# A transformer layer on one core: another way to the largest |k| of the first key block, with V copies and LayerNorm means moved between engines

## The chip, the cores and the metric

One core of a Trainium2 chip. The time is that of one execution in device microseconds; "before" is the median of three runs, 922.26 us (922.0 to 924.7). The durations quoted come from one profiled execution of 922.3 us, whose traced span is 920.3 us.

The engines by the names of the profile: PE is TensorE (PEld its weight loads), DVE is VectorE, ACT is ScalarE, POOL is GpSimd, SP is SyncE, which issues the DMAs here. All run their own instruction streams in order and wait for each other by semaphores.

## What is computed

One pre-norm transformer layer on 2048 tokens of width 640, in bfloat16: attention with 32 heads of 20 columns, then a gated feed-forward block of width 1728.

```python
h  = x + attention(layernorm(x), wqkv, wo)       # 32 heads, softmax over 2048 keys
h2 = h + (gelu(layernorm(h) @ w_gate) * (layernorm(h) @ w_up)) @ w_down

def attention(x, wqkv, wo):
    q, k, v = split(x @ wqkv)                    # each 2048 x 640
    p = softmax(q @ k.T * 20 ** -0.5)            # per head
    return concat(p @ v) @ wo
```

## The kernel before

**Planned order.** The kernel doesn't write out the order of its instructions. Every operation is handed to a planner (`Sched`, lines 44 to 295) with its engine, an estimated length, a priority, what it reads and writes, and the PSUM banks it takes and frees. The planner runs through time once and lets each free engine take the ready operation of the best priority; TensorE also gets filler matmuls where its recent load would be low. What comes out is one fixed stream per engine, with semaphore waits. So a changed length, priority or bank list can move instructions of all engines. Its estimates stand at the operations (`c_act(512)`, `c_dve(512)`, 0.33 and the like).

**Stages.** The work goes in three stages.

1. *Front.* x is loaded in four parts of four 128-token tiles. LayerNorm 1 (`ln_stats`, `act_stats`, `ln_rsqrt`, `ln_apply`, lines 532 to 633) gets mean and variance of a tile, on VectorE for three parts and on ScalarE for the second; `ln_rsqrt` rounds them to bfloat16 (`mv16`), adds epsilon (`sd16`), copies the mean to `mu`, takes a square root on ScalarE and a reciprocal (`rs`) on VectorE; `ln_apply` writes (x - mu) * rs on VectorE; `transposes` turns the tile over by five matmuls with the identity and copies it out of PSUM to `xnT`, on ScalarE except for tiles 13 and 15, which VectorE copies. Then come the projections. `proj_k(t)` makes block t of K (128 of the 640 columns, transposed, 6.4 heads) in four chunks c of 512 keys, five matmuls each; `proj_q(t, c)` the same for 512 queries; `proj_v(kt, hf)` the V rows of 128 keys for 16 heads.
2. *Attention.* Scores of four heads at a time (a head group), a tile of 128 keys x 512 query columns per head; ScalarE takes three or two such tiles in one exponential of 1536 or 1024 columns out of PSUM (lines 928 to 947); VectorE makes a few of the exponentials itself by arithmetic (`d_exp`, lines 833 to 873); TensorE sums over keys with V (`pv_op`, line 875). Queries go in seven parts of 512 to 128. K and Q blocks 1 to 4 and most of V are made during the first part, beside its exponentials.
3. *After each part of queries*: output projection, LayerNorm 2, feed-forward; for the last part nothing runs beside it (the tail).

**The bound on the scores.** The exponential needs a number to be subtracted per query. The kernel uses a bound: for each head the sum over its 20 rows of |q| times the largest |k| of that row over all keys. `kd[:, t]` holds this largest |k| of block t, `sel` a selector matrix (which row belongs to which head), scaled by `kd`. For the first block (t = 0) `sel0` takes the place of `sel`, and `q_bound0` (lines 749 to 759) multiplies it with |q| (line 752) and adds the result onto the q rows in `qt_all` (line 756). The first score matmul waits for that, and so does the first exponential.

In `proj_k(0)` (lines 674 to 714) each chunk is copied out of PSUM by ScalarE (line 667). VectorE then masks the sign bits of the copy (line 689), takes the running maximum of the chunks elementwise (line 694, from the second chunk on), after the last chunk halves the 512 columns to 256 by one more maximum (line 697), reduces these to one column (line 708) and scales `sel0` (line 711) and `sel` (line 713). For later blocks the masking is done once over 2048 columns and the halving goes 1024, 512, 256.

`proj_v(kt, 0)` is handed over for all 16 key tiles, in banks 6 and 7, its copies out of PSUM on VectorE (lines 1168 and 1169); the first four have a better priority than the others. K blocks from 1 on are copied on VectorE (line 670).

Most operations are recorded through the helper `I`, so their line in the profile is 354.

Of the kernel before, what the change touches and what calls it, by code (L numbers as in the profile page):

```python
# [7 lines left out]
ALU = mybir.AluOpType  # L8
# [291 lines left out]
D = 640  # L300
# [32 lines left out]
def bass_sequential_preLN__mha_block__glu_gated_geglu__prompt_kernel(  # L333
# [12 lines left out]
    with ExitStack() as es:  # L346
# [33 lines left out]
        sd16 = sb("sd16", [128, NT])  # L380
        nw = sb("nw", [128, 2, 4], FP32)
        kd = sb("kd", [128, NA], FP32)
        kt_all = sb("kt_all", [128, NG, S])
        qt_all = sb("qt_all", [128, 4, NG, 512])
        v_all = sb("v_all", [128, NT, H, VW])
# [142 lines left out]
        q_fills = [["qf0%d" % g for g in range(1, NG, 2)], ["qf1"], ["qf2"], ["qf3%d" % g for g in range(0, NG, 2)]]  # L528

        e_ops = []  # L530

        def ln_stats(src, t, rkeys, prio, after=()):
            s = t % 4
# [8 lines left out]
        def ln_rsqrt(t0, n, prio, table=False, sqrt=False):  # L542

            y = rs[:, t0:t0 + n]
            a, b = nw[:, 0, 0:n], nw[:, 1, 0:n]
            ts = range(t0, t0 + n)
            k16, ks = ("mv16", t0), ("sd16", t0)
            rk = [("rs", t) for t in ts]
            v = lambda fn, r, w: op("dve", fn, 0.17, prio, reads=r, writes=w)
            d = v if table or sqrt else lambda fn, r, w: op(POOL, fn, 0.25, prio, reads=r, writes=w)  # L550
            d(I("tensor_copy", mv16[:, t0:t0 + n, :], mv[:, t0:t0 + n, :]), [("mv", t) for t in ts], [k16])
            d(I("tensor_scalar", sd16[:, t0:t0 + n], mv16[:, t0:t0 + n, 1], LN_EPS, None, ALU.add), [k16], [ks])
            d(I("tensor_copy", mu[:, t0:t0 + n], mv16[:, t0:t0 + n, 0]), [k16], [("mu", t) for t in ts])
            if sqrt:
                op("act", I("activation", sd16[:, t0:t0 + n], sd16[:, t0:t0 + n], ACT.Sqrt), 0.2, 1, reads=[ks], writes=[ks])
                v(I("reciprocal", y, sd16[:, t0:t0 + n]), [ks], rk)
                return
            if table:
                op("act", I("activation", sd16[:, t0:t0 + n], sd16[:, t0:t0 + n], ACT.Sqrt), 0.2, -1, mode="sqrt", reads=[ks],
                   writes=[ks])  # L560
                v(I("reciprocal", y, sd16[:, t0:t0 + n]), [ks], rk)
                return
            d(I("tensor_copy", a, sd16[:, t0:t0 + n]), [ks], ["nw0"])
            d(I("tensor_scalar", y.bitcast(I32), a.bitcast(I32), -0.5, RSQRT_MAGIC, ALU.mult, ALU.add), ["nw0"], rk)
            for _ in range(2):
                d(I("tensor_tensor", b, y, y, ALU.mult), rk, ["nw1"])
                d(I("tensor_tensor", b, b, a, ALU.mult), ["nw0", "nw1"], ["nw1"])
                d(I("tensor_scalar", b, b, -0.5, 1.5, ALU.mult, ALU.add), ["nw1"], ["nw1"])
                d(I("tensor_tensor", y, y, b, ALU.mult), ["nw1"] + rk, rk)
            d(I("tensor_tensor", sd16[:, t0:t0 + n], a, y, ALU.mult), ["nw0"] + rk, [ks])  # L570
            v(I("reciprocal", y, sd16[:, t0:t0 + n]), [ks], rk)

        def ln_apply(eng, src, dst, dkey, t, rkeys, prio):
            if eng == "act":
                fn = I("activation", dst, src, ACT.Identity, bias=nm[:, t:t + 1], scale=rs[:, t:t + 1])
            else:
                fn = I("tensor_scalar", dst, src, mu[:, t:t + 1], rs[:, t:t + 1], ALU.subtract, ALU.mult)
            return op(eng, fn, 0.82 if eng == "act" else c_dve(D, 0.46), prio,
                      reads=list(rkeys) + [("mu", t), ("rs", t)] + ([("nm", t)] if eng == "act" else []), writes=[dkey])

        def transposes(src, rkeys, dst, wkey, banks, prio, evac, after=()):
# [40 lines left out]
        for t0 in (0, 4, 8, 12):  # L622
            if t0 == 4:
                act_stats(4, 4)
            else:
                for t in range(t0, t0 + 4):
                    ln_stats(x_sb[:, t, :], t, [f"x{t // 4}"], 1.4 if t0 == 12 else P_BG)
            ln_rsqrt(t0, 4, P_PRO, sqrt=True)
            for t in range(t0, t0 + 4):
                e_ops.append(ln_apply("dve", x_sb[:, t, :], xn_p[:, t % 4, :], ("xnp", t % 4), t, [f"x{t // 4}"], P_PRO))  # L630
                transposes(xn_p[:, t % 4, :], [("xnp", t % 4)], xnT[:, :, t * 128:(t + 1) * 128], ("xnT", t),
                           ALLB, P_PRO, "dve" if t in (13, 15) else "act")
                e_ops.append(len(sc.ops) - 2)


        w_readers = []

        def chain(bk, key, n, steps, reads, prio, acq=True, after=()):
            for k, (l, r) in enumerate(steps):
# [17 lines left out]
                w_readers.append(i)  # L657
            return i

        def proj_qk(col, t, c, dst, dkey, banks, prio, evac, after=()):  # L660
            bk = Bank(*banks)
            key = ("bk", sc_id())
            w_readers.extend(chain(bk, key, 512, [(wqk[:, a, col + 128 * t:col + 128 * t + 128],
                                                   xnT[:, a, c * 512:(c + 1) * 512]) for a in range(NA)],
                                   [("xnT", tt) for tt in range(4 * c, 4 * c + 4)] + ["wqk"], prio))
            if evac == "act":
                e = op("act", lambda eng: eng.activation(dst, bank(bk), ACT.Copy), c_act(512), prio, reads=[key],
                       writes=[dkey], rel=[bk])
            else:
                e = op("dve", lambda eng: eng.tensor_copy(dst, bank(bk)), c_dve(512), prio, reads=[key],  # L670
                       writes=[dkey], rel=[bk], after=after)
            w_readers.append(e)

        def proj_k(t, banks, prio, evac="dve"):
            for c in range(4):
                src = k_un[t % 2][:, 512 * c:512 * c + 512]
                proj_qk(D, t, c, src, ("ku", t % 2, c), banks, prio, evac, after=e_ops if t == 1 else ())
                if t == 0:
                    for j in range(4):
                        k_keys[0][c].append(("k", 0, c, j))  # L680
                        dma(kt_all[32 * j + 1:32 * j + 21, 0, 512 * c:512 * c + 512],
                            src[DH * j:DH * j + DH, :], ("k", 0, c, j), [("ku", 0, c), "ktm0"],
                            f"kc{c}", 2.2, prio)
                dma(kdr[128 * t:128 * t + 128, 512 * c:512 * c + 512], src, ("kdr", t, c), [("ku", t % 2, c)], f"kw{t % 2}{c}", 2.7,
                    max(prio, P_BG) if t == 0 else prio, 0.4)
                if t == 0 or c == 3:
                    c0 = c if t == 0 else 0
                    n = 512 * (c + 1 - c0)
                    w_readers.append(op("dve", I("tensor_scalar", ka[:, 512 * c0:512 * c + 512].bitcast(I16),
                                                 k_un[t % 2][:, 512 * c0:512 * c + 512].bitcast(I16), 0x7FFF, None, ALU.bitwise_and),  # L690
                                        0.066 + n * 0.00026, prio, reads=[("ku", t % 2, cc) for cc in range(c0, c + 1)],
                                        writes=[("ka", cc) for cc in range(c0, c + 1)]))
                if t == 0 and c:
                    op("dve", I("tensor_tensor", ka[:, 0:512], ka[:, 0:512], ka[:, 512 * c:512 * c + 512], ALU.max), 0.33, prio,
                       reads=[("ka", 0), ("ka", c)], writes=[("ka", 0)])
            for n in (256,) if t == 0 else (1024, 512, 256):
                op("dve", I("tensor_tensor", ka[:, 0:n], ka[:, 0:n], ka[:, n:2 * n], ALU.max), 0.066 + n * 0.00052, prio,
                   reads=[("ka", c) for c in range(4)], writes=[("ka", c) for c in range(4)])
            if t:
                g0, g1 = STEP[t]  # L700
                for j in range(4):
                    for g in range(g0, g1):
# [2 lines left out]
                    dma(kt_all[32 * j + 1:32 * j + 21, g0:g1, :],  # L705
                        kdr.rearrange("(g j e) s -> j e g s", j=4, e=DH)[j, :, g0:g1, :], ("k", t, j),
                        [("kdr", tt, c) for tt in (t - 1, t) for c in range(4)] + k_fill, f"k{t}", 2.2 + 1.0 * (g1 - g0), prio, keep=False)
            op("dve", I("tensor_reduce", kd[:, t:t + 1], ka[:, 0:256], AX.X, ALU.max), 0.33, prio, reads=[("ka", 0)],
               writes=[("kd", t)])
            if t == 0:  # L710
                op("dve", I("tensor_scalar", sel0[:, :, 0], sel[:, 0, 0:4], kd[:, 0:1], None, ALU.mult), 0.1, prio,
                   reads=["sel", "sel0", ("kd", 0)], writes=["sel0"])
# [36 lines left out]
        def q_bound0(banks, prio):  # L749
# [3 lines left out]
                bank(bk), sel0[:].rearrange("p j e -> p (j e)"), aq[0], start=True, stop=True),  # L753
                c_mm(512), prio, mode="full", util=0.213, reads=[("aq", 0), "sel0"], writes=[key], acq=[bk]))
            dst = qt_all[:, 0, 0, :]
            op("dve", lambda eng: eng.scalar_tensor_tensor(out=dst, in0=bank(bk), scalar=off0[:, 0:1], in1=dst,
                                                           op0=ALU.add, op1=ALU.add), c_dve(512) + 0.05, prio,
               reads=[key, "off0"] + q_keys[0][0], writes=[("qo", 0, 0)], rel=[bk])
            q_keys[0][0] = [("qo", 0, 0)]

        def proj_v(kt, hf, banks, prio, evac="dve"):
# [404 lines left out]
        sc.warm_bank = 7  # L1166
        sc.warm_deps = tuple(sc.lw[kk] for kk in k_keys[0][0])
        for kt in range(NT):
            proj_v(kt, 0, (6, 7), P_EPI if kt < 4 else P_BG, "dve")
        
        ui = 0
        for s_, (c, gs) in enumerate(slots):
# [66 lines left out]
```

## Time and profile before

| What | Value |
|---|---|
| median of three runs | 922.26 us (922.0 to 924.7) |
| profiled execution: time, span | 922.3 us, 920.3 us |
| granted TensorE clock | 1.0 in all stretches |
| first exponential starts | 35.37 us |
| last exponential ends | about 885 us |
| ACT busy in the span | 875.9 us in 783 instructions |
| PE busy / DVE busy / POOL busy | 847.7 / 795.2 / 41.4 us |
| one exponential of 1536 columns / 1024 columns | 1.51 / 1.10 us (mean) |
| K chunk copied by ACT (128x512) / by DVE | 0.64 / 0.69 us (mean) |
| V copy by DVE (128x320) | 0.49 us (mean) |
| reduce 128x256 to one column on DVE | 0.41 us, five times |

How to read it: a row of a timeline gives start, length, engine, line, operation, what is written <- what is read, the number of instructions run together, and in brackets how long the engine had been idle and who ended that. Lengths of neighbours overlap a little, since the next instruction starts while the last one writes back. A matmul's length is from its start to its modelled end; the next one starts earlier.

### The profile page before, as it was taken

What the parts mean: (1) busy time and instruction counts of PE and PEld (TensorE: products, weight loads), DVE (VectorE), ACT (ScalarE), POOL (GpSimd) and SP (SyncE); (2) the same over time, 40 slices, a digit from 0 to 9 for tenths busy, and PEclk for the clock granted to TensorE, in tenths of its full rate; (3) what the DMA queues carried; (4) which work ended last, traced back from release to release, by engine and by line L of the source; (5) the groups of instructions that cost most, each with busy time, mean ns of one, the idle gap of its engine ahead of it and who ended that gap; (6) DMA issues with size and microseconds to landing.
All of it is one profiled execution on the core that took longest, in us unless ns stands there. A gap on an engine that the chain in (4) does not pass through costs nothing.

```text
span 920.3 us, 23148 instructions
## 1 busy us (share of the span) xinstructions
PE 847.7 (92%) x10202; PEld 356.0 (39%) x10202; DVE 795.2 (86%) x1468; ACT 875.9 (95%) x783; POOL 41.4 (5%) x117
## 2 busy tenths in 40 slices
PE   3999999999898887989998998999999999999998
PEld 2432223222232222223333333344444445666577
DVE  8869898999799996988888999899999888878763
ACT  7899999999999999999999999999999999999961
POOL 5000000000001000000001000000202000100200
PEclk9999999999999999999999999999999999999999
DMA  7311020223801000000122000001120102000000
GB/s 258 94 25 38 12 61 25 84 78 85 293 6 30 1 2 1 1 1 16 44 31 30 2 1 1 1 16 30 22 39 1 16 9 38 17 17 24 10 16 16
DMA packets 39516, 34.36 MB, mean 37 GB/s; under 512 B 19436, under 2 KB 36936, under 8 KB 39416
## 3 DMA queue, kind: packets, MB, share of 16 engines
q1 hardware_dynamic: 39416, 32.89, 13.2%
q8 instruction: 80, 1.31, 0.6%
q14 instruction: 20, 0.16, 0.1%
HBM read 20.12 MB, written 8.09 MB: 31 GB/s over the span
## 4 chain that ended last, share of the span: by engine, by line
ACT 51%; PE 34%; DVE 12%; DMA 1%; issue 0%; SPq 0%; DVEq 0%
ACT pts L354 32%; ACT rege L354 18%; PE ps L917 10%; PE ps L354 7%; PE ps L1089 6%; PE ps L640 6%; DVE qt_all L354 5%; PE ps L1146 4%; DVE qt_all L852 2%; DVE rege L354 2%; DMA regw<-in_A_wqkv_dram 1%; DVE rege L852 1%; ACT L354 1%; PE ps L1012 1%; PE ps L585 1%
## 5 line engine op out<-in xcount | busy, mean ns | idle before, releaser
L354 ACT ACTIVATE pts<-ps 128x1536 bf16<-128x1536 f32 (+1 forms) x471 | 559.3, 1316 | 7.7 <-PE ps L917 5.4
L917 PE MATMUL ps<-qt_all,kt_all 32*128 32x256 bf16 (+2 forms) x3584 | 321.1, 288 | 37.7 <-ACT pts L354 22.8
L354 ACT ACTIVATE rege<-ps 128x1536 bf16<-128x1536 f32 (+1 forms) x232 | 284.9, 1314 | 2.1 <-PE ps L354 1.4
L917 PEld LDWEIGHTS ps<-qt_all,kt_all 32*128 32x128 bf16 x3584 | 104.4, 92 | 259.7 <-ACT pts L354 134.0
L354 DVE TENSOR_TENSOR qt_all<-qt_all 128x2048 f16<-128x2048 f16 (+3 forms) x186 | 175.0, 941 | 2.2
L1089 PE MATMUL ps<-rege,regw 128*128 128x256 bf16 (+2 forms) x980 | 160.9, 290 | 9.9 <-ACT rege L354 3.4
L354 PE MATMUL ps<-pts,v_all 128*21 128x256 bf16 (+2 forms) x2080 | 122.5, 290 | 0.0
L852 DVE TENSOR_SCALAR qt_all<-ps 128x512 int16<-128x512 f32 x128 | 87.7, 685 | 27.2 <-PE ps L917 26.9
L852 DVE TENSOR_SCALAR rege<-ps 128x512 int16<-128x512 f32 x128 | 87.7, 685 | 15.3 <-PE ps L917 14.2
L1089 PEld LDWEIGHTS ps<-rege,regw 128*128 128x128 bf16 x980 | 71.9, 97 | 70.7 <-issue 28.7
L354 PE MATMUL ps<-rege,v_all 128*21 128x256 bf16 (+2 forms) x1204 | 94.5, 295 | 0.2 <-DVE qt_all L354 0.2
L640 PE MATMUL ps<-regw 128*128 128x512 bf16 (+1 forms) x360 | 86.3, 350 | 2.3 <-DMA regw<-in_A_wqkv_dram 0.7
L354 DVE TENSOR_SCALAR qt_all<-qt_all 128x1024 f16<-128x1024 int16 (+2 forms) x153 | 85.0, 560 | 1.8
L1146 PE MATMUL ps<-regw,rege 128*128 128x320 bf16 x448 | 79.0, 301 | 1.7 <-DVE rege L1135 0.6
L354 DVE TENSOR_TENSOR rege<-rege 128x1024 f16<-128x1024 f16 (+4 forms) x106 | 67.4, 647 | 0.9
L354 PE MATMUL ps<-kt_all,zer 128*32 128x512 bf16 x784 | 63.7, 384 | 0.0
L354 PEld LDWEIGHTS ps<-pts,v_all 128*21 128x21 bf16 x2080 | 45.0, 91 | 32.9 <-issue 28.8
L1146 PEld LDWEIGHTS ps<-regw,rege 128*128 128x128 bf16 x448 | 37.3, 97 | 33.8 <-issue 16.2
L354 DVE TENSOR_SCALAR rege<-rege 128x1024 int16<-128x1024 int16 (+2 forms) x117 | 49.2, 443 | 0.9
L1135 DVE TENSOR_TENSOR rege<-rege,ps 128x512 bf16<-128x512 bf16 (+1 forms) x53 | 35.7, 677 | 14.3 <-PE ps L1089 14.1
L640 PEld LDWEIGHTS ps<-regw 128*128 128x128 bf16 x360 | 28.7, 98 | 47.2 <-issue 21.9
L354 PEld LDWEIGHTS ps<-rege,v_all 128*21 128x21 bf16 x1204 | 32.4, 91 | 24.0 <-issue 17.4
(101 smaller groups left out, 563.3 us busy)
## 6 DMA issues: line engine op xcount, KB each, us to landing
rege<-in_A_x_dram SPq DMA_DIRECT2D x6, 640.0 KB, 5.1
q_rows<-regw SPq DMA_DIRECT2D x20, 128.0 KB, 1.7
out_dram<-rege SPq DMA_DIRECT2D x16, 160.0 KB, 1.8
regw<-in_B_w_gate_dram SPq DMA_DIRECT2D x1, 2160.0 KB, 8.1
regw<-in_B_w_up_dram SPq DMA_DIRECT2D x1, 2160.0 KB, 14.5
regw<-in_B_w_down_dram SPq DMA_DIRECT2D x1, 2080.0 KB, 19.7
kt_all<-k_rows SPq DMA_DIRECT2D x12, 160.0 KB
qt_all<-q_rows SPq DMA_DIRECT2D x12, 160.0 KB
```

The costliest lines, as they stand in the source:

```text
L354: return lambda eng: getattr(eng, method)(*args, **kwargs)
L585: op("pe", lambda eng, a=a: eng.transpose(bank16(bk, D)[:, 128 * a:128 * a + 128], src[:, a * 128:(a + 1) * 128], ident[:]), 0.055, prio, ...
L640: yield op("pe", lambda eng, l=l, r=r, k=k: eng.matmul(bank(bk, n), l, r, start=(k == 0), stop=(k == len(steps) - 1)), c_mm(n), prio, mode ...
L852: d_ops.append(op("dve", lambda eng: eng.tensor_scalar(v[:, 512 * h:512 * h + 512], bank(b), EXP_MUL, -32000.0, ALU.mult, ALU.max), c_dve( ...
L917: return lambda eng: eng.matmul(out()[:, kk * nq:(kk + 1) * nq], kt_all[32 * j:32 * j + 32, g, kt * 128:(kt + 1) * 128], qt_all[32 * j:32 ...
L1012: op("pe", lambda eng, tt=tt: eng.transpose(bank(b2)[:, tt * 128:(tt + 1) * 128], osb[:, s, tt * 128:(tt + 1) * 128], identf[:]), c_mm(128 ...
L1089: op("pe", lambda eng, a=a, f=f, fi=fi: eng.matmul(bank(bk)[:, fi * nq:(fi + 1) * nq], w[:, a, F0[f]:F0[f] + 128], hnT[:, a, 128 * tb:128 ...
L1135: hdone.append(op("dve", lambda eng, bu=bu, fv=fv, w=w: eng.tensor_tensor(fv, fv, bank(bu, w), ALU.mult), c_dve(w), p, reads=[ku] + hkeys( ...
L1146: op("pe", lambda eng, f=f, o=o, hf=hf, bk=bk: eng.matmul(bank(bk, 320), ha_f[:, o:o + 128], wd[:, f, hf * 320:(hf + 1) * 320], start=(f = ...
```

## The change

- `proj_k(0)`: VectorE takes the largest |k| of each chunk at once, by one `tensor_reduce` over 512 columns with absolute values, into a column of the new `kd4`. Chunks 0 to 2 are read from ScalarE's copy in SBUF, chunk 3 straight from PSUM, and ScalarE's copy of chunk 3 now comes after that reduce. A reduce over the four columns gives `kd[:, 0]`. The masking, the running maximum and the halving go for block 0; blocks 1 to 4 keep theirs.
- `proj_v(kt, 0)`: bank 5 may be used besides 6 and 7, and the first four copies go to ScalarE.
- LayerNorm 1: `mu` is now -mean, made by a multiplication on GpSimd instead of a copy on VectorE; `ln_apply` adds it instead of subtracting. LayerNorm 2 is as before.
- Names for constants (`C_POOL`, `T_POOL`, `T_DVE`, `q_first`) come without an effect: `T_POOL` is empty, `T_DVE` holds 13 and 15 as before.

```diff
         kd = sb("kd", [128, NA], FP32)
+        kd4 = sb("kd4", [128, 4], FP32)
...
-            d(I("tensor_copy", mu[:, t0:t0 + n], mv16[:, t0:t0 + n, 0]), [k16], [("mu", t) for t in ts])
+            if sqrt:
+                op(POOL, I("tensor_scalar", mu[:, t0:t0 + n], mv16[:, t0:t0 + n, 0], -1.0, 0.0, ALU.mult, ALU.add), 0.25, prio, reads=[k16],
+                   writes=[("mu", t) for t in ts])
+            else:
+                d(I("tensor_copy", mu[:, t0:t0 + n], mv16[:, t0:t0 + n, 0]), [k16], [("mu", t) for t in ts])
...
-        def proj_qk(col, t, c, dst, dkey, banks, prio, evac, after=()):
+        def proj_qk(col, t, c, dst, dkey, banks, prio, evac, after=(), peak=None):
...
+            def top(src, r):
+                return op("dve", lambda eng: eng.tensor_reduce(kd4[:, c:c + 1], src(), AX.X, ALU.max, apply_absolute_value=True),
+                          c_dve(512), prio, reads=[r], writes=[("kd4", c)])
+            if peak and c == 3:
+                after = (top(lambda: bank(bk), key),)
             if evac == "act":
                 e = op("act", lambda eng: eng.activation(dst, bank(bk), ACT.Copy), c_act(512), prio, reads=[key],
-                       writes=[dkey], rel=[bk])
+                       writes=[dkey], rel=[bk], after=after)
...
+            if peak and c < 3:
+                w_readers.append(top(lambda: dst, dkey))
...
-                if t == 0 or c == 3:
-                    c0 = c if t == 0 else 0
-                    n = 512 * (c + 1 - c0)
+                if t and c == 3:
+                    c0 = 0
+                    n = 2048
...
-                if t == 0 and c:
-                    op("dve", I("tensor_tensor", ka[:, 0:512], ka[:, 0:512], ka[:, 512 * c:512 * c + 512], ALU.max), 0.33, prio,
-                       reads=[("ka", 0), ("ka", c)], writes=[("ka", 0)])
-            for n in (256,) if t == 0 else (1024, 512, 256):
+            for n in (1024, 512, 256) if t else ():
...
+            else:
+                op("dve", I("tensor_reduce", kd[:, 0:1], kd4[:], AX.X, ALU.max), 0.12, prio, reads=[("kd4", c) for c in range(4)],
+                   writes=[("kd", 0)])
...
-            proj_v(kt, 0, (6, 7), P_EPI if kt < 4 else P_BG, "dve")
+            proj_v(kt, 0, (6, 7, 5), P_EPI if kt < 4 else P_BG, "act" if kt < 4 else "dve")
```

## The prediction

> **What bounds the kernel now.** I read the page's totals and slices first, then the busy time in five stretches, then the timeline of the 18 us ahead of the first exponential, then the rows around ScalarE's longest later wait. The totals line and the ScalarE row of the slices:
>
> ```profile
> PE 847.7 (92%) x10202; PEld 356.0 (39%) x10202; DVE 795.2 (86%) x1468; ACT 875.9 (95%) x783; POOL 41.4 (5%) x117
> ...
> ACT  7899999999999999999999999999999999999961
> ```
>
> Busy time by stretch (columns: length, then PE, PEld, DVE, ACT, POOL, clock, DMA share, GB/s):
>
> ```profile
> 17.00:35.40 18.40, 18.13 (x134) 10.20 (x134) 16.75 (x57) 10.95 (x21) 0.00 (x0) 1.00 0.22 68
> 35.40:140.00 104.60, 100.30 (x817) 32.05 (x816) 89.41 (x181) 103.55 (x91) 0.00 (x0) 1.00 0.15 44
> 140.00:200.00 60.00, 57.16 (x452) 16.55 (x451) 54.92 (x112) 58.11 (x52) 0.00 (x0) 1.00 0.23 66
> 200.00:885.00 685.00, 637.84 (x8366) 268.72 (x8367) 605.11 (x1045) 681.57 (x586) 29.30 (x85) 1.00 0.11 27
> 885.00:920.30 35.30, 31.75 (x422) 26.51 (x418) 15.52 (x36) 8.10 (x12) 0.00 (x0) 1.00 0.06 20
> ```
>
> From the first exponential (35.37) to the last (about 885) ScalarE is idle for only 1.05 + 1.89 + 3.43 us. So the time is: start of the first exponential, plus a fixed load of exponentials, plus a few stalls, plus a tail of 35 us. The change touches only what lies ahead of about 240 us: set side by side, the instruction streams of the two kernels are equal on VectorE from instruction 461 of 1470 on, on TensorE from 1766 of 10,204, on SP from 126 of 180; ScalarE's differ only ahead of the first exponential, with all 703 exponentials and 14 table loads the same. So two things can move: the start of the first exponential, and ScalarE's stalls up to 200 us (1.05 + 1.89 = 2.94 us).
>
> The rows ahead of the first exponential (start, length):
>
> ```profile
> 27.29 6.42 PE L640 MATMUL ps<-regw 128*128 128x512 bf16 x33
> ...
> 29.79 0.60 ACT L667 ACTIVATE regw<-ps 128x512 bf16<-128x512 f32 x1 [0.39 <-PE ps L640]
> ...
> 30.75 0.28 DVE L354 TENSOR_SCALAR rege<-regw 128x512 int16<-128x512 int16 x1
> ...
> 31.06 0.43 DVE L354 TENSOR_TENSOR rege<-rege 128x512 bf16<-128x512 bf16 x1
> ...
> 31.86 0.28 DVE L354 TENSOR_TENSOR rege<-rege 128x256 bf16<-128x256 bf16 x1
> ...
> 32.10 0.69 DVE L670 CAST rege<-ps 128x512 bf16<-128x512 f32 x1
> 32.70 0.41 DVE L354 TENSOR_REDUCE kd<-rege 128x1 f32<-128x256 bf16 x1
> 33.15 0.24 DVE L354 TENSOR_SCALAR sel<-sel,kd 128x4 bf16<-128x4 bf16 x1
> 33.31 0.69 DVE L670 CAST rege<-ps 128x512 bf16<-128x512 f32 x1
> ...
> 33.54 0.38 PE L752 MATMUL ps<-regw,sel 128*128 128x512 bf16 x1
> ...
> 34.07 0.75 DVE L756 SCALAR_TENSOR_TENSOR qt_all<-ps,off,qt_all 128x512 bf16<-128x512 f32 x1
> ...
> 35.37 4.62 ACT L354 ACTIVATE pts<-ps 128x1536 bf16<-128x1536 f32 x4 [3.68 <-PE ps L917]
> ```
>
> Two chains end together at the bound matmul (L752, 33.54). One is VectorE's: the last K chunk's copy ends at 30.39, then mask, maximum, halving, reduce, scaled selector (33.15). The other is TensorE itself: from 17.27 it starts a matmul every 0.216 us (128x512), 0.136 (128x320) or 0.056 (transpose). Ahead of L752 stand 42, 21 and 60 of them: 9.07 + 2.86 + 3.36 = 15.29 of the 16.27 us; the other 0.98 us is mostly a slow start of the first six. **TensorE's stream is full**, so shortening VectorE's chain alone would bring nothing; what counts is which matmuls now stand ahead of L752.
>
> **Step 1: the bound matmul.** In the new stream 36 instead of 42 matmuls of 512, 20 instead of 21 of 320 and the same 60 transposes stand ahead of it: 6 x 0.216 + 0.136 = 1.43 us less, at best 32.11.
>
> **Step 2: VectorE's new chain.** It needs three reduces from SBUF (chunks 0 to 2), one from PSUM (chunk 3), one of four columns. No row shows a 512-wide reduce. Low end: the 256-wide row, 0.41. High end: twice it, 0.82. Nearest: CAST 128x512 out of PSUM, 0.69 against 0.49 for 320, so 1.03 ns a column; 0.41 + 256 x 1.03 ns = 0.67, which I take for all four, with the next starting 0.07 earlier, as the rows around it do (0.60 a piece). The four-column one: 0.11 to 0.24 by the small VectorE rows; I take 0.15.
>
> The Trainium skill speaks against this: "VectorE: DVE Perf Modes", section "Rules for kernel authors", calls `tensor_reduce` on a hot path the slowest VectorE operation and says to restructure. The rows agree on the single instruction, not on the sum: the pair it replaces, mask 0.28 and maximum 0.43, occupies as much as one reduce of 0.67. By the rule alone the step loses, and the sum goes the way of the dear reduce; by the rows it is even.
>
> When do they run? Chunk 1's and 2's copies stand on ScalarE behind the ten transposed copies. Their first transposes start behind four matmuls of 320 more and one of 512 less: 21.79 + 4 x 0.136 - 0.216 = 22.12, so 0.33 us later; one 0.10 us square root no longer stands between them: chunk 1's copy moves from 28.21 to 28.44 and ends at 29.04. Reduces: 29.08, 29.68, 30.28. The last needs chunk 3's last matmul: 25 of 512 and 20 of 320 ahead, so 33.54 - 17 x 0.216 - 0.136 = 29.73, plus 0.42 for matmul and signal: 30.15, in time. VectorE then copies block 1's first K chunk, which TensorE ends at 33.54 - 13 x 0.216 - 0.136 + 0.42 = 31.01; 0.60 later the four-column reduce (31.61), 0.04 of signal, the selector at **31.80** (33.15 before). The two constraints, TensorE's 31.01 and VectorE's 30.88, lie 0.13 us apart. At 0.82 a reduce, the copy slips to 31.30 and all that follows by 0.29; at 0.41 nothing is won, since the copy waits for TensorE.
>
> From the selector on: matmul 0.39 later, 32.19 (step 1 allows 32.11); its output 0.42 later, 32.61; but VectorE still has the full selector and one K copy ahead of the fused add: 31.80 + 0.27 + 0.15 + 0.60 = 32.83 (before: 33.15 + 0.92). Then 1.30 as before (34.07 to 35.37): **first exponential at 34.13 instead of 35.37, 1.24 us earlier**; with the dear reduce 0.95.
>
> **Covered edits.** The first chunk's reduce now stands ahead of the group's reciprocals, which run at 21.1 instead of 20.60; the first normalized tile is then there at 21.75, and TensorE reaches its transposes at 22.12: cover 0.37 us; beyond it each us is paid in full. Four V copies on ScalarE: 0.60 for 512 columns, 0.70 for 640, so about 0.43 each; two lie in idle time ahead of the transposed copies (0.30 + 0.71 us idle there), two behind chunk 2's copy, where 3.68 us were idle. The third bank adds no instruction. The negated means on GpSimd:
>
> ```profile
> L354 POOL TENSOR_TENSOR rs<-rs,nw 128x1 f32<-128x1 f32 x2 | 1.9, 949 | 0.2
> L354 POOL CAST mu<-mv 128x2 f32<-128x2 bf16 x3 | 1.6, 544 | 0.0
> ```
>
> So 0.2 to 1.2 us for a few numbers. Two of them, queued from about 19.4, must end before the first normalized tile of the second group (21.4): 0.4 to 2.4 us, hidden up to 2.0, and the excess lies inside the same 0.37 us of cover. On SP, the writing of block 1's first chunk (0.40) goes behind the twelve K loads; the loads of the next groups, issued at 43.18, are first needed past 60. "SBUF — State Buffer", "Who interferes with whom", has it that a GpSimd instruction and a VectorE one in a two-port mode lock each other out for a whole instruction; the stretched GpSimd rows fit that. By it VectorE could also lose 0.2 us four times, which no row here shows.
>
> **Step 3: the stalls up to 200 us.** The largest:
>
> ```profile
> 137.84 2.83 PE L640 MATMUL ps<-regw 128*128 128x320 bf16 x14
> ...
> 141.04 2.37 ACT L354 ACTIVATE pts<-ps 128x1024 bf16<-128x1024 f32 x2 [1.40 <-PE ps L917]
> ```
>
> Fourteen V matmuls stand in TensorE's queue ahead of a score unit (number 91), each fifth waiting for a bank that VectorE frees between other work. In the new stream at most seven stand together there (ahead of unit 92), so this 1.40 should go. Against it, the new start leaves arrears: 5 x 0.216 + 0.136 = 1.22 us of TensorE work now lie behind the first score unit, and a K copy on VectorE. That makes a wait likelier at the end of a head group, where the last sum over keys waits for VectorE's exponentials; the row of that kind at 194.3 costs 0.75. I put one more such wait at 0.75 to 1.5, take 1.1, and get -0.30 in sum. Bounds: all 2.94 gone, or two waits of 1.40 more.
>
> **Sum.** The profiled execution took 922.3 (span 920.3 and 2.0 around it; the median of the runs is 922.26). 922.3 - 1.24 - 0.30 = **920.8**.
>
> **Rivals.**
> - *Reduce at 0.82, stalls as they were*: 922.3 - 0.95 = 921.4. Chance 0.14.
> - *The front doesn't move* (the change doesn't do what it says: V copies and late reciprocals hold up the transposed copies as much as the chain is shortened): 922.3, or 922.0 with the stalls of step 3. For it: ScalarE's ten copies run without a gap. Against it: they start only 0.33 later. 0.08.
> - *All early stalls vanish*: 922.3 - 1.24 - 2.94 = 918.1. 0.06.
> - *Slower: the arrears become head-of-line waits.* A queue of V or K matmuls waits for VectorE ahead of a score unit, as at 139.6, at the ends of head groups 3, 4 and 5: 922.3 - 1.24 + 3 x 1.40 = 925.3; with two, 923.9. It decides once the waits added pass 1.24 us. For it: TensorE is 96% and VectorE 85 to 92% busy there. 0.08.
> - *Forecast* 920.8: 0.64.
>
> About 0.3% (2.8 us) is what a measurement of this kernel can tell from no change: faster means below 919.5, which the vanished stalls and the forecast's lower edge reach (0.07); slower means above 925.0, the full case of the arrears (0.04); the rest 0.89. The range takes in the dear reduce, the unmoved front and one added wait above (922.9), and half of the stalls gone below (919.2).
>
> **What would show it.** First exponential at 33.9 to 34.5; the L752 matmul's successor near 32.2; 512-wide reduces of 0.6 to 0.75; no idle TensorE of over 0.2 us from 22 to 32; ScalarE's idle from the first exponential to 200 us at 1.5 to 4 us; all after 240 us shifted as a block. A first exponential past 35, or a wait of over 2 us at a group's end, would make the prediction wrong.

## The result and the profile after

The changed kernel takes **920.95 us** (median of 14 runs, 920.42 to 921.32) against 922.83 (921.57 to 926.95) of the kernel before beside it: ratio 0.9978, 95% interval 0.9969 to 0.9987. Its profiled execution took 921.06 with a span of 919.1; that of before 922.3 with 920.3. The medians differ by 1.9 us, the two profiled executions, both at a granted clock of 1.00, by 1.2: in the later comparisons about half of the executions of the kernel before had a granted clock below 1.00, mostly 0.998, and a longer time (last section). The forecast was 920.8. The time came out; the way to it did not, as the rows show.

The slice row of ScalarE and the busy time by stretch (columns as in the prediction):

```profile
ACT  6899999999999999999999999999999999999961
```

```profile
17.00:35.40 18.40, 18.06 (x128) 9.80 (x128) 14.72 (x48) 13.23 (x27) 0.54 (x3) 1.00 0.19 58
35.40:140.00 104.60, 100.99 (x798) 32.62 (x798) 90.94 (x184) 104.52 (x93) 0.00 (x0) 1.00 0.16 46
140.00:200.00 60.00, 58.00 (x449) 16.94 (x448) 55.95 (x115) 58.08 (x52) 0.00 (x0) 1.00 0.26 69
200.00:884.00 684.00, 635.16 (x8358) 268.00 (x8353) 604.02 (x1041) 680.70 (x586) 29.30 (x85) 1.00 0.10 27
```

ScalarE's idle time is 0.08 + 1.92 us up to 200 us (1.05 + 1.89 before) and 3.30 behind it (3.43). The stall of 1.40 at 139.6 is gone, and so are the ones of 0.40 at 42.3 and 0.75 at 194.3. Two are new:

```profile
143.00 2.37 ACT L354 ACTIVATE rege<-ps 128x1536 bf16<-128x1536 f32 x2 [0.57 <-PE ps L354]
...
169.32 1.45 ACT L354 ACTIVATE pts<-ps 128x1536 bf16<-128x1536 f32 x1 [1.35 <-PE ps L354]
```

Both are released by TensorE's sums over keys (PE L354). One by one, the waits of over 0.05 us up to 200 us come to 1.97 us against 2.94: **0.97 less**.

The front, in the rows that answer those of before:

```profile
18.56 4.94 PE L649 MATMUL ps<-regw 128*128 128x512 bf16 x20 [0.24 <-ACT regw L598]
...
23.42 0.80 PE L592 MATMUL ps<-ident,rege 128*128 128x128 bf16 x10
...
29.75 1.20 ACT L682 ACTIVATE regw<-ps 128x512 bf16<-128x512 f32 x2
...
30.49 1.28 DVE L677 TENSOR_REDUCE kd<-regw 128x1 f32<-128x512 bf16 x2 [1.06 <-ACT regw L682]
...
31.69 0.68 DVE L677 TENSOR_REDUCE kd<-ps 128x1 f32<-128x512 f32 x1
...
33.07 0.51 DVE L354 TENSOR_SCALAR sel<-sel,kd 128x4 bf16<-128x4 bf16 x2
...
33.38 0.38 PE L770 MATMUL ps<-regw,sel 128*128 128x512 bf16 x1
...
35.42 1.45 ACT L354 ACTIVATE pts<-ps 128x1536 bf16<-128x1536 f32 x1 [1.12 <-PE ps L935]
```

The new chain has the lengths that were taken for it (each of the four reduces takes 0.68 or 0.69 and the next starts 0.60 later; selector to first exponential 2.35), but everything in it stands 1.3 us late: the second group's transposes start at 23.42 (forecast 22.12), the copies at 29.75 (28.44), the selector at 33.07 (31.80). The first exponential, **35.42**, is where it was before (35.37). So of the 1.2 us by which the span is shorter, the front brought nothing, the stalls up to 200 us 0.97, and small differences behind 200 us the rest.

Why the transposes are late is seen in TensorE's weight loads (columns: start, length). Ahead of each 128x512 matmul one is loaded, and the rows stand 0.43 us apart until 21.1, where they run together:

```profile
20.24 0.15 PEld L649 LDWEIGHTS ps<-regw 128*128 128x128 bf16 x1 [0.28 <-issue]
20.67 0.15 PEld L649 LDWEIGHTS ps<-regw 128*128 128x128 bf16 x1 [0.28 <-issue]
21.10 2.07 PEld L649 LDWEIGHTS ps<-regw 128*128 128x128 bf16 x13 [0.28 <-issue]
```

In the kernel before they run together from 19.03 on:

```profile
18.72 0.15 PEld L640 LDWEIGHTS ps<-regw 128*128 128x128 bf16 x1 [0.28 <-issue]
19.03 2.50 PEld L640 LDWEIGHTS ps<-regw 128*128 128x128 bf16 x14 [0.17 <-issue]
```

Up to there a 512-column matmul starts every 0.427 us, from there every 0.216: TensorE runs its first projections at half speed, though the granted clock stands at 1.00. In the kernel before this phase ended at 18.72. Each output column issued in it costs 0.427/512 - 0.216/512 = 0.41 ns more. Between the first projection (17.10) and the end of the phase stand 4352 columns, before (from 17.27) 1792: 2560 x 0.41 ns = **1.05 us**; by the starts of the single matmuls the phase cost 1.74 us against 0.79, 0.95 more.

The rest of the lateness is ScalarE's. TensorE waits for its copies ahead of the matmul at 18.56 (0.71 us between two starts in place of 0.27, so 0.44 lost) and again at 23.2 (0.09 lost); its first projection starts 0.17 earlier: 0.95 + 0.53 - 0.17 = 1.31 us. These parts are not what could be saved one by one: at full speed the wait ahead of 18.56 would grow by the 0.48 us that the four matmuls before it lose to half speed.

### The profile page after: what moved, and what is told of

Its sections match the earlier page's. It is cut to its first block, busy times and chain, and to the rows that moved or that the text cites. A ratio compares the mean times of both kernels' runs of the same rounds, so it can differ in the third digit from the quotient of the medians.

```text
span 919.1 us, 23058 instructions
## 1 busy us (share of the span) xinstructions
PE 846.4 (92%) x10159; PEld 355.6 (39%) x10159; DVE 794.5 (86%) x1456; ACT 877.0 (95%) x787; POOL 42.1 (5%) x121
## 3 DMA queue, kind: packets, MB, share of 16 engines
q1 hardware_dynamic: 39416, 32.89, 12.9%
q8 instruction: 80, 1.31, 0.6%
## 4 chain that ended last, share of the span: by engine, by line
ACT 62%; PE 27%; DVE 11%; issue 1%; DVEq 0%
ACT pts L354 39%; ACT rege L354 22%; PE ps L935 8%; PE ps L1107 6%; PE ps L354 5%; DVE qt_all L354 4%; PE ps L1164 4%; PE ps L649 3%; DVE qt_all L870 2%; ACT L354 1%; DVE rege L870 1%; DVE stats L354 1%; PE ps L592 1%; PE ps L1030 1%; DVE rege L354 1%
## 5 line engine op out<-in xcount | busy, mean ns | idle before, releaser
L354 ACT ACTIVATE pts<-ps 128x1536 bf16<-128x1536 f32 (+1 forms) x471 | 559.3, 1318 | 3.5 <-PE ps L935 1.5
L354 ACT ACTIVATE rege<-ps 128x1536 bf16<-128x1536 f32 (+1 forms) x232 | 285.2, 1317 | 2.6 <-PE ps L354 2.0
L354 DVE TENSOR_TENSOR qt_all<-qt_all 128x2048 f16<-128x2048 f16 (+3 forms) x186 | 174.9, 940 | 2.2
L354 PE MATMUL ps<-pts,v_all 128*21 128x256 bf16 (+2 forms) x2080 | 122.6, 290 | 0.0
L354 PE MATMUL ps<-rege,v_all 128*21 128x256 bf16 (+2 forms) x1204 | 94.9, 295 | 0.3
L354 DVE TENSOR_SCALAR qt_all<-qt_all 128x1024 f16<-128x1024 int16 (+2 forms) x153 | 84.9, 559 | 1.8
L354 DVE TENSOR_TENSOR rege<-rege 128x1024 f16<-128x1024 f16 (+4 forms) x102 | 66.0, 657 | 1.0
L354 PE MATMUL ps<-kt_all,zer 128*32 128x512 bf16 x736 | 60.6, 384 | 0.0
L354 PEld LDWEIGHTS ps<-pts,v_all 128*21 128x21 bf16 x2080 | 44.9, 91 | 33.3 <-issue 29.3
L354 DVE TENSOR_SCALAR rege<-rege 128x1024 int16<-128x1024 int16 (+2 forms) x117 | 50.2, 447 | 1.1
L1153 DVE TENSOR_TENSOR rege<-rege,ps 128x512 bf16<-128x512 bf16 (+1 forms) x53 | 35.7, 676 | 14.3 <-PE ps L1107 14.1
L354 PEld LDWEIGHTS ps<-rege,v_all 128*21 128x21 bf16 x1204 | 32.4, 91 | 24.7 <-issue 16.8
```

The source lines that it names most:

```text
L354: return lambda eng: getattr(eng, method)(*args, **kwargs)
L1153: hdone.append(op("dve", lambda eng, bu=bu, fv=fv, w=w: eng.tensor_tensor(fv, fv, bank(bu, w), ALU.mult), c_dve(w), p, reads=[ku] + hkeys( ...
```

## The experiments

All are planned anew as a whole, so each kernel's order differs in places other than its edit. "Full speed from" below is the start of the first matmul whose distance to the next is nearer to that of full speed; "columns" are the output columns of projections issued ahead of it.

**Is the half-speed phase the same in each execution?** Both kernels again, unchanged.

> The kernel before, unchanged, in a new execution. In both profiles TensorE starts its first matmuls at half speed (a 128x512 every 0.43 us instead of 0.216): until 19.0 us in the profile before, until 21.1 us in the profile after. Theory A (the switch to full speed falls at another time in each execution; the change shortens the front by 1.24 us at an equal switch): the first exponential starts at 35.4 + 0.5 x (switch - 19.0), and the switch is not at 19.0 again. Theory B (the switch is set by the kernel's own order, and the change moved it): switch at 19.0 and first exponential at 35.4 as before, within 0.1 us.

> The changed kernel, unchanged, in a new execution. Theory A: first exponential at 34.1 + 0.5 x (switch - 19.0), with a switch that is not at 21.1 again. Theory B: switch at 21.1 and first exponential at 35.4 again. Both: waits of ScalarE at 142.4 (0.57) and 168.0 (1.35) as in the profile after, shifted with the front, and none of over 0.3 us at 139.6.

Measured: before 922.18, full speed from 19.38 (2816 columns), first exponential 35.60. After 921.12, full speed from 21.02 (4352), first exponential 35.42, the same stalls as in its first profile. So one program's phase can differ by 0.7 us from execution to execution, and the changed kernel's did not.

**The phase taken away.** 19 filler matmuls (128x512, into bank 5) from the landing of x on:

```diff
+        for k in range(9):
+            fb = Bank(5)
+            n = 3 if k < 5 else 1
+            op("pe", [I("matmul", PS[:, 512 * 5:512 * 6], ident[:], kt_all[:, 0, 0:512], start=True, stop=True, skip_group_check=True)] * n,
+               0.4 * n if k < 5 else 0.215, 8, mode="full", reads=["ident", "ktm0", "x0"], acq=[fb], rel=[fb],
+               after=() if k < 5 else (tr0[0],))
```

> The kernel before with 19 filler matmuls of 128x512 on TensorE between the landing of x and the first projection, in PSUM bank 5, which nothing else uses then; all other instructions keep their order. They should bring TensorE to full speed before 17 us. Theory A: no half-speed matmul after 17 us, 0.85 us saved in the first six projections, first exponential at 34.4 to 34.6, time 0.9 us below the kernel before. Theory B: the same.

> The changed kernel with the same fillers. Theory A: first exponential 1.2 to 1.3 us ahead of that of the kernel before with fillers, at 33.1 to 33.4; time 2.9 to 3.2 us below the kernel before (0.95 of the fillers, 1.24 of the front, 1.0 of fewer waits from there to 200 us). Theory B (ScalarE's later copies hold the front up whatever the clock): first exponential less than 0.3 us ahead of the other one with fillers, and the time 1.9 to 2.1 below.

Measured: with fillers, before 922.14 (ratio to before 0.9992, 0.9983 to 1.0001), projections at full speed from 17.09, first exponential 34.40. After with fillers 922.61 (1.0004, 0.9992 to 1.0016), first exponential 34.61. Theory A is not met: the changed front is no shorter even so. The phase was not quite gone there: TensorE ran at half speed again from 15.8 to 18.8, which cost the first four projection matmuls 0.48 us, less than half of the 1.2 that theory A asks for. And it stood idle 0.41 us at 17.4 for ScalarE's transposed copies, the last of which ended at 18.34 (17.27 in the kernel before with fillers). So the phase alone is not the whole answer: something had made ScalarE's front late. Its rows in the changed kernel:

```profile
12.31 0.74 ACT L354 ACTIVATE rege<-rege 128x640 bf16<-128x640 bf16 x1
...
14.59 0.70 ACT L598 ACTIVATE regw<-ps 128x640 bf16<-128x640 bf16 x1 [1.46 <-PE ps L592]
```

and in the variant with the means on VectorE:

```profile
13.02 0.74 ACT L354 ACTIVATE rege<-rege 128x640 bf16<-128x640 bf16 x1
...
14.32 0.70 ACT L594 ACTIVATE regw<-ps 128x640 bf16<-128x640 bf16 x1 [0.47 <-PE ps L588]
```

A pass over a tile of x (128x640, for the second group's sums) stands ahead of the first transposed copy in the variant (13.02) and behind it in the changed kernel (15.19). There ScalarE idles 1.46 us ahead of the copy, and the later copies come late.

**The means back on VectorE, all else as changed.**

```diff
-            if sqrt:
-                op(POOL, I("tensor_scalar", mu[:, t0:t0 + n], mv16[:, t0:t0 + n, 0], -1.0, 0.0, ALU.mult, ALU.add), 0.25, prio, reads=[k16],
-                   writes=[("mu", t) for t in ts])
-            else:
-                d(I("tensor_copy", mu[:, t0:t0 + n], mv16[:, t0:t0 + n, 0]), [k16], [("mu", t) for t in ts])
+            d(I("tensor_copy", mu[:, t0:t0 + n], mv16[:, t0:t0 + n, 0]), [k16], [("mu", t) for t in ts])
...
-                fn = I("tensor_scalar", dst, src, mu[:, t:t + 1], rs[:, t:t + 1], ALU.add if first else ALU.subtract,
+                fn = I("tensor_scalar", dst, src, mu[:, t:t + 1], rs[:, t:t + 1], ALU.subtract,
                        ALU.mult)
```

> The changed kernel with LN1's means put back on VectorE; new maximum, V copies on ScalarE and third bank stay. In the written order of ScalarE's queue its third sum pass over the second 512 rows (before the first xnT copy) stands again ahead of that copy, as in the kernel before; in the changed kernel it stands behind it, and ScalarE idled 1.46 us there. Theory C (that one place in the queue makes ScalarE's front about 1 us late and keeps TensorE longer in its half-speed phase): half speed until about 19.5 us instead of 21.0, first exponential at 34.0 to 34.4 us instead of 35.42, the three early stalls of the changed kernel unchanged (0.05, 0.57, 1.35), time about 919.8 (1.2 below the changed kernel). Theory D (the length of the half-speed phase has its own cause and does not hang on this place): half speed until 21, first exponential at 35.3 to 35.5, time 921.

Measured: 920.32 (ratio to before 0.9971, 0.9960 to 0.9982); first exponential 35.07, stalls 0.06, 0.57, 1.35 as foreseen; but full speed only from 21.39, with 5376 columns ahead of it. The place in the queue was restored (idle 0.47) and gave 0.35 us; the phase was not shortened by it. Theory C holds for the place and falls for the phase; the time lies between the two forecasts. To set this kernel against the changed one on one chip, both ran once more:

> The changed kernel, a third profile and times beside its variant on one chip. Theory G (the moment at which TensorE comes to full speed is fixed by a kernel's instructions): full speed from 21.0 to 21.1 us again, first exponential 35.4. Theory H (it differs from execution to execution): full speed from anywhere between 18.5 and 21.5 us and the first exponential between 34.2 and 35.5 with it. Time 920.6 to 921.2.

> The changed kernel with the means on VectorE, beside the changed kernel on one chip. Theory C: 0.4 to 0.9 us below the changed kernel in the median. Rival (the means cost nothing, the difference of 0.6 was one of chips): within 0.3 of it. Full speed: theory G at 21.4 us again with the first exponential at 35.07; theory H anywhere between 18.5 and 21.5 with the first exponential between 33.9 and 35.1.

Measured: changed kernel 921.05 (920.73 to 921.24, five runs; ratio to before 0.9969, 0.9957 to 0.9981), full speed from 21.09, first exponential 35.42. With the means on VectorE 920.04 (919.53 to 920.49, five runs; 0.9959, 0.9947 to 0.9971), full speed from 20.33 (3840 columns), first exponential 34.67. The two ranges don't touch: **the means on GpSimd cost about 1 us here** (0.6 by the medians of the other runs). For theory G the changed kernel speaks (three profiles within 0.08 us), for H this variant (21.39 and 20.33). Rows of the second profile, beside those of the changed kernel above:

```profile
28.80 1.19 ACT L678 ACTIVATE regw<-ps 128x512 bf16<-128x512 f32 x2
...
34.67 1.45 ACT L354 ACTIVATE pts<-ps 128x1536 bf16<-128x1536 f32 x1 [1.34 <-PE ps L931]
```

**The means alone, and the place in the queue alone.** First the kernel before with only the edit of the means; then the kernel before, means untouched, with two passes put behind the first copies:

```diff
                     op("act", I("activation", junk, x_sb[:, t, :], f, accum_out=asum[:, k, t - t0:t - t0 + 1]), 0.86, 1.4,
-                       reads=[f"x{t // 4}"], writes=["junk", ("as", t)])
+                       reads=[f"x{t // 4}"], writes=["junk", ("as", t)],
+                       after=(copies[k],) if t == 7 else ())
...
+                copies.append(len(sc.ops) - 1)
```

> The kernel before with only the edit of the means: LN1's means negated on GpSimd. The third sum pass falls behind the first xnT copy here too. Theory C: ScalarE idles about 1.4 us at 13 us, half speed until about 21, first exponential at 36.3 to 37 instead of 35.37 to 35.60, stalls as in the kernel before (2.9), time 923.2 to 924. Theory D: first exponential within 0.3 of the kernel before, time 922.3 to 922.6.

> The kernel before with one thing moved: the seventh and eighth sum passes of ScalarE stand behind the first and second xnT copies, as in the changed kernel. Theory C (this place alone costs the front): ScalarE idles about 1.3 us at 13 us, first exponential at 36.0 to 36.9 us depending on the half-speed phase, time 922.9 to 924.1. Rival (the place does not matter, the copies behind it have slack): first exponential 35.2 to 35.7, time 922.0 to 922.7.

Measured: means alone 923.24 (1.0008, 0.9999 to 1.0016), idle 1.46, full speed from 18.97 (1792 columns), first exponential 35.93; a little less late than expected, since the phase was short. Place alone 923.66 (1.0006, 0.9997 to 1.0015), idle 1.33, 18.42 (1600 columns), first exponential 36.06. In both medians lie above the 922.62 and 923.00 of before, though the intervals of the ratio just reach 1. Those medians of before mix executions at a granted clock of 1.0 and below; its executions at 1.0 beside them have medians of 921.74 and 921.77, those of the two variants 923.24 and 923.61, 1.5 and 1.8 us more. The profiles say the same: with no more columns at half speed than before, the first exponential is 0.56 and 0.69 us later. The place by itself does it (with what the planner moves along with it).

The means also delay the first normalized tile. GpSimd's queue (POOL) and VectorE, in the changed kernel:

```profile
13.07 2.39 POOL L354 MEMSET qt_all<- 128x512 f32 x4
13.18 0.61 DVE L354 TENSOR_SCALAR rege<-rege,mu,rs 128x640 bf16<-128x640 bf16 x1
```

In the kernel before:

```profile
12.15 2.41 POOL L354 MEMSET qt_all<- 128x512 f32 x4
...
13.12 0.39 DVE L354 TENSOR_SCALAR rege<-rege,mu,rs 128x640 bf16<-128x640 bf16 x1
```

The negated mean ahead of them pushes GpSimd's four memsets 0.9 us back, and one now starts 0.1 us ahead of the tile, which takes 0.61 in place of 0.39. The tiles of the same form ahead of which no memset starts within 0.2 us take 0.39 to 0.45 in both kernels, those with one 0.51 to 0.61. The Trainium skill, "SBUF — State Buffer", "Who interferes with whom", has a VectorE instruction in a two-port mode and a GpSimd one shut each other out for a whole instruction; the rows agree in direction, at 0.1 to 0.2 us each. Whether these tiles run in such a mode no row shows, and that the memset is the cause was not tried by itself.

**The V edit alone**: the kernel before with the one line of `proj_v` changed.

```diff
-            proj_v(kt, 0, (6, 7), P_EPI if kt < 4 else P_BG, "dve")
+            proj_v(kt, 0, (6, 7, 5), P_EPI if kt < 4 else P_BG, "act" if kt < 4 else "dve")
```

> The kernel before with only the V edit: the first four V copies on ScalarE, third bank for V. If the stall of 1.40 at 139.6 us went because V's products no longer pile up behind VectorE's copies, it is gone here without the new maximum: first exponential at 35.3 to 35.6, stalls 1.2 to 1.5 in place of 2.9, time 921.0 to 921.4. Rival (the new maximum, which frees VectorE by about 3.6 us, took the stall away): the stall of 1.40 stays and ScalarE's copies come 0.4 late, time 922.3 to 922.7.

Measured: 921.87 (0.9989, 0.9979 to 1.0000). The stall of 1.40 is gone without the new maximum; the stalls up to 200 us come to 1.1, those to 221 us to 1.3. First exponential 35.82, later than expected, with 3328 columns at half speed (full speed from 19.88). So the theory holds for the stall. The time lies between the two that were expected: the front of this profile was 0.45 us longer, and seven of the eleven executions had a granted clock of 0.996 to 0.999. The four at 1.0 have a median of 921.1, which the theory gave, against 921.74 of before at 1.0.

**The new maximum alone**: the changed kernel with V copies and means as before.

> The changed kernel with V copies back on VectorE (two banks) and means back on VectorE: the new maximum alone. Theory (a shorter front needs V's products out of the way in time): first exponential at 34.0 to 34.4, but V's products are put late and ScalarE waits for them, 8 to 11 us in all around 56 and 121 us: time 927 to 931. Rival (the new maximum stands by itself): first exponential 34.2, stalls 2.9 as before, time 921.0.

Measured: 930.80 (1.0082, 1.0066 to 1.0099). ScalarE's longest new waits are 6.09 and 3.43 us. The first, with TensorE's row ahead of it:

```profile
63.50 3.71 ACT L354 ACTIVATE pts<-ps 128x1536 bf16<-128x1536 f32 x3 [6.09 <-PE ps L354]
```

```profile
59.78 0.85 PE L645 MATMUL ps<-regw 128*128 128x320 bf16 x5 [0.55 <-DVE v_all L787]
60.98 1.93 PE L645 MATMUL ps<-regw 128*128 128x512 bf16 x10 [0.34 <-DVE regw L681]
```

TensorE works off V and K projections, waiting for VectorE to free their banks, ahead of the sums over keys that the exponential needs. First exponential 35.09 (34.0 to 34.4 expected) with 5376 columns at half speed. The new maximum by itself, in the order that is planned for it, costs 8 us; the V edit is what makes it usable here.

**The front at full speed**: fillers in the changed kernel with the means on VectorE.

> The changed kernel with the means on VectorE, plus the 19 filler matmuls of the two warmed kernels. They keep TensorE at full speed when its first projection starts at 17.0 us, so the length of the half-speed phase drops out. Theory E (a front's length is that of its own order of work plus about 0.41 ns for each output column issued at half speed): first exponential at 32.9 to 33.5 us, 0.9 to 1.5 ahead of the warmed kernel before (34.40). Theory F (the new maximum does not shorten the front, something else is late): 34.2 to 34.6. The fillers' own effect on the whole time is not what is tested: both warmed kernels ran at a granted clock of 0.991 to 0.998 and gave their early start back; time 919.5 to 922.

Measured: 921.28 (0.9968, 0.9955 to 0.9981); first exponential 33.57, against 34.40 of the kernel before with fillers. The two rows, the variant first:

```profile
33.57 3.71 ACT L354 ACTIVATE pts<-ps 128x1536 bf16<-128x1536 f32 x3 [1.33 <-PE ps L940]
```

```profile
34.40 2.37 ACT L354 ACTIVATE pts<-ps 128x1536 bf16<-128x1536 f32 x2 [3.68 <-PE ps L926]
```

0.83 us: just short of what theory E gives, and far from F. The fillers were not clean here either: from 14.3 to 17.3 TensorE went back to half speed, with fifteen transposes and part of the first projection matmul in it.

**All unwarmed profiles together**, the last column being the first exponential less 0.41 ns a column:

| kernel | full speed from | columns | first exponential | less the phase |
|---|---|---|---|---|
| before | 18.72 / 19.38 | 1792 / 2816 | 35.37 / 35.60 | 34.64 / 34.45 |
| V edit alone | 19.88 | 3328 | 35.82 | 34.46 |
| means alone | 18.97 | 1792 | 35.93 | 35.20 |
| place alone | 18.42 | 1600 | 36.06 | 35.40 |
| changed (three) | 21.02 to 21.09 | 4352 | 35.42 | 33.64 |
| changed, means on VectorE | 21.39 / 20.33 | 5376 / 3840 | 35.07 / 34.67 | 32.87 / 33.10 |
| new maximum alone | 21.45 | 5376 | 35.09 | 32.89 |

The last column sorts them: about 34.5 without the new maximum, 33.0 with it, and 0.5 to 1.0 more wherever the pass stands behind the copy. It takes off too much where TensorE would have waited anyway (the changed kernel ahead of 18.56 and at 23.2), so its differences are upper ends, about 1.5 us for the new maximum; the pair with fillers gives the lower one, 0.83.

## Why the prediction was right in the time and wrong in its steps

- **What bounds the kernel**: right. The span moved by the first exponential's start and the stalls up to 200 us; behind 200 us it moved by some 0.3 us only.
- **Step 1, the bound matmul at 32.19**: wrong, 33.38. The count of matmuls was right; the speed was not. The step that failed here is the sentence that puts 0.98 us down to "a slow start of the first six". It was read as a fixed cost. It is a phase of half speed: it held 1792 and 2816 columns in the kernel before and 3840 to 5376 in those with the new maximum, and took 0.95 us more in the changed kernel than in the one before. What should have been priced is a range: 0.4 and 0.6 us between two executions of one kernel, about 1.5 us over all profiles (1600 to 5376 columns).
- **Step 2, VectorE's chain**: the sizes were right. Reduces 0.68 to 0.69 from SBUF and 0.68 from PSUM (0.67 taken), the next 0.60 later (0.60 taken); four columns 0.15 (0.15 taken); selector to first exponential 2.35 (2.33 taken). The Trainium skill's rule against `tensor_reduce` decided nothing: one reduce cost what mask and maximum had (0.28 and 0.43). The chain began late, with the copies. First exponential 35.42 in place of 34.13: the forecast said that past 35 it would be wrong, and in this step it was. With the 1792 columns of the kernel before it would stand at about 34.4, by the table's correction, an estimate. A front shorter by 1.24 us lies between the two ends that the runs give for the new maximum with the V edit, 0.83 and about 1.5, once the means are back on VectorE.
- **Covered edits**: the first two V copies held as costed (0.43 and 0.44), the other two took 0.58 and 0.59 but started 0.32 apart. The late reciprocals ran at 22.14 (21.1 forecast), and the first normalized tile of the second group was done at 23.28, 0.14 us ahead of its transposes (0.37 forecast). What was said of the **means** did not hold. The instructions took 0.19 us and were hidden, as said; what was not looked at is what the edit moved: ScalarE's pass went behind the first copy, and GpSimd's memsets slid beside the first normalized tile. That is 0.35 to 0.75 us in the first exponential, 0.6 to 1.0 in the time. The prediction's own view that ScalarE's streams "differ only ahead of the first exponential" named the very place and went no further.
- **Step 3, the stalls**: the mechanism was right, the 1.40 went, and through the V edit as its run alone shows. The size was off: -0.97 in place of -0.30. Two waits on sums over keys came (0.57 and 1.35, where 1.1 was put), but 0.75, three of 0.10 to 0.15 and most of 0.40 went as well.
- **The sum**: -1.24 and -0.30 were forecast, about 0, -0.97 and -0.3 came. The two errors cancel: the time came out by luck. Of the rivals "the front doesn't move" was right in that the front did not move, but not in the cause it named, the V copies and late reciprocals: a V copy held the transposes up by 0.09 us at 23.2, the half-speed phase and the misplaced pass did the rest. It was wrong in the time it gave, 922.0, since it left the stalls too dear.

What stays open: what sets the end of the half-speed phase. All five unwarmed profiles without the new maximum have it at 18.4 to 19.9, all six with it (counting the variants) at 20.3 to 21.5, yet TensorE's instructions up to its end are nearly the same. Whether the change itself lengthens it, no run here decides.

## What to carry to other kernels

Before a count of matmuls is turned into time, look at how far apart they start: the first ones after an idle stretch may run at half speed, and how many do is not the kernel's alone to say. An edit that is cheap and hidden may still move another engine's queue; set the two orders side by side ahead of the point that matters, and ask of each swapped pair which of the two is ready first. A shorter front is worth nothing if what was pushed behind it (here V) is needed soon after. The best version seen is the change without its edit of the means, 920.04 and 920.32.

## What the runs showed of the hardware

- **Half speed with a granted clock of 1.00.** 512-column matmuls start 0.427 us apart, then 0.216; transposes 0.11, then 0.056. The fillers, issued back to back, began so too, for 3.0, 2.1 and 4.2 us in the three kernels that have them. The clock row of the profile shows nothing of it. The Trainium skill, "TensorE: Matmul & The Clock Gate", "What's actually happening", tells of such a gate with a free-running window of about 3.4 us and counts that vary from run to run. The factor of two between the spacings agrees, and so does the spread over executions of two kernels; that three profiles of the changed kernel agree within 0.08 us is not what a free window alone would lead one to expect.
- **Fillers cost later what they win.** All 31 runs with the 19 fillers had a mean granted clock of 0.991 to 0.998. In the profile of the kernel before with fillers, a wait of 1.35 us that it lacks otherwise stands at 301 us, where the granted clock was 0.74 from 300 to 305 us: the first exponential was 1.0 us earlier and the span 0.3 longer. Such a dip is not the fillers' alone: the profile of the place alone, without them, has 0.66 in the same 5 us, with a wait of 0.99.
- **A granted clock of 0.998 without fillers.** The kernel before had it in 10 of 17 runs of the last comparison, with a median of 924.4 against 921.77 in its seven runs at 1.0. The changed kernel had it in one of 20 runs. At 1.0 the two stand at 921.77 and 921.05 there, 0.7 us apart; the rest of the difference of the medians comes with the clock. Why the one meets it more often is not shown.
